# Start addresses of the MLP's weight blocks, modulo 256 bytes, in an attention and MLP kernel on one core

## The chip, the cores and the metric

The kernel runs on one core of a Trainium2 chip. The metric is the device time in microseconds (us) of one execution. Engines are named as the profile names them: PE is the matrix engine's matmul, PEld its weight load, DVE, ACT and POOL are the vector, scalar and GpSimd engines, SP issues DMAs. SBUF is the on-chip memory of 128 partitions; an address here is a byte offset inside a partition.

## What is computed

Eight batches of eight attention heads (576 positions, head size 64), half of the heads with a plain window of 32, half with a dilated one, feed an MLP with 4608 tokens, model size 512 and inner size 2048:

```python
def _attn_ref(q, k, v):
    scores = scale * np.matmul(q, k.transpose(0, 1, 3, 2))
    mask_plain = (rel >= 0) & (rel < window)                                  # window 32
    mask_dil = (rel >= 0) & (rel < window * dilation) & (rel % dilation == 0)  # dilation 4
    scores = np.where(masks[None, :, :, :], scores, -1000000000.0)
    attn = np.exp(scores - np.max(scores, axis=-1, keepdims=True))
    attn = attn / (np.sum(attn, axis=-1, keepdims=True) + 1e-09)
    return np.matmul(attn, v).astype(np.float32)

def _moe_ref(x, w_in, w_out):
    h = x @ w_in
    g = np.where(h >= 1, h, np.where(h <= -1, 0.0, (h + 1) ** 2 / 4.0))
    return (g @ w_out).astype(np.float32)
```

The weights arrive as 64-bit floats.

## The kernel before, in words

The MLP takes nearly all of the time. Its tokens are cut into 9 tiles of 512, its inner size into 16 blocks of 128. One pair (token tile t, inner block f) is a step; there are 144 steps, and `steps` lists them with f running fastest. A step has two parts on PE:

- `layer1` (matmuls on line 670): 4 chunks of 128 model rows, 3 matmuls each. The stationary operand is a piece of 128 columns of block `wi{f}`, the moving operand is 512 columns of the token tile `xh` or `xl`. Every operand is in the fp32r type and split into a high and a low part, so that one product takes three matmuls: high times high, low weight times high token, high weight times low token.
- `layer2` (line 726): 4 blocks of 128 tokens, 3 matmuls each. Here the activations `gh` and `gl` are stationary (128 columns), and the block `wo{f}` is moving (512 columns).

So each step has 24 matmuls of 512 columns, each with a weight load of 128 columns of its own, and 144 steps have 3,456 of them. Between the two parts, DVE and ACT make the activations of a step (`clamped`, `squared`, `activated`, `g_high`, `g_low`, lines 678 to 697); `layer2` runs two steps behind `layer1`, so that PE does not wait for them. Attention of later batches is worked in between steps: score matmuls (`scores_split`, line 336) with a stationary operand of 96 columns from `qs` and a moving one of 256 columns from `kk`, and the values matmuls (line 628). They come from the table `slots`; the first 18 steps and the first heads are in an order written out by hand, `OPENING`, which holds for all engines.

The weights stay in SBUF for the whole run: 32 blocks, `wi0` to `wi15` and `wo0` to `wo15`, of 4,096 bytes in each partition. `fetch` (line 188) allocates a block's place and loads the raw 64-bit numbers from SP; five conversion operations on ACT, DVE and POOL (`scaled`, `low_bits`, `joined`, `high_part`, `low_part`) turn it in place into two fp32r parts. Before a block is fetched, seventeen of the places serve early heads (`home`, `borrow`).

Where a tile lies follows from the sizes of the tiles allocated ahead of it, rounded up to 32 bytes. In the kernel before, almost every tile is a multiple of 256 bytes long (`kr` is 32 numbers longer than it need be; the two tiles `c` of line 282 have 32 numbers beyond the scores, of which 18 are used, and are 3,200 bytes long each, 6,400 together). As a result every block `wi` and `wo`, every token tile `xh` and `xl`, and `gh`, `gl`, `kk` and `qs` begin at 64 modulo 256.

Below, the distance of a matmul pair is the start of a stationary operand minus the start of the moving operand that streams while it is loaded, modulo 256. Pieces inside a tile lie at multiples of 512 bytes, so for the matmuls of `layer1` and `layer2` the distance is 0 throughout. In a score block the second weight load (384 bytes on) stands at 128 to the moving operand of the first matmul.

Of the kernel before, what the change touches and what calls it, by code (L numbers as in the profile page):

```python
# [23 lines left out]
F32 = mybir.dt.float32  # L24
F32R = mybir.dt.float32r
U32 = mybir.dt.uint32
# [5 lines left out]
DM, DF = 512, 2048  # L32
WIN, DIL = 32, 4
QT, NQ = 96, 6
# [62 lines left out]
def body(ctx, tc, q, k, q2, k2, v, v1, fixed_in, w_in, w_out, out):  # L97
# [4 lines left out]
    pool = ctx.enter_context(tc.tile_pool(name="pool", bufs=1))  # L102
# [16 lines left out]
    home = {  # L119
# [3 lines left out]
    }  # L123

    def borrow(name):
        return pool.tile([128, 2 * DM], F32, tag=home[name], name=f"{name}_place")

    first_tiles = 3
    first_q, first_k = first_tiles * QT, first_tiles * QT + 32
# [8 lines left out]
    def load_q(n):  # L138
        if f"q{n}" in home:
            qr = borrow(f"q{n}")[:, :S]  # L140
        else:
            tag = "qs" if n < native and n % 4 else "qr"
            qr = pool.tile([128, S], F32, tag=tag, name=f"qr{n}")
        if n < native:
            some = slice(0, first_q if n == 0 else S)
            nc.sync.dma_start(out=qr[:, some], in_=q[n // 2][:, some])
            whole["q", n] = qr
            for j in range(2):
                heads[n + j]["qs"] = qr[64 * j : 64 * j + 64]
        else:  # L150
            nc.sync.dma_start(out=qr, in_=q2[n - native])
            heads[n]["qr"] = qr

    def load_k(n):
        if f"k{n}" in home:
            kr = borrow(f"k{n}")[:, :KPAD]
        else:
            tag = "kk" if n < native and n % 4 else "kr"
            kr = pool.tile([128, KPAD + 32], F32, tag=tag, name=f"kr{n}")[:, :KPAD]
        if n < native:  # L160
            some = slice(0, first_k if n == 0 else KPAD)
            nc.sync.dma_start(out=kr[:, some], in_=k[n // 2][:, some])
            whole["k", n] = kr
            for j in range(2):
                heads[n + j]["ks"] = kr[64 * j : 64 * j + 64]
        else:
            nc.sync.dma_start(out=kr, in_=k2[n - native])
            heads[n]["kr"] = kr
# [3 lines left out]
    def load_v(n):  # L172
        width = 2 * NQ * (D + 1 if n in late else D)
        if f"v{n}" in home:
            vt = borrow(f"v{n}")[:, :width]
        else:
            vt = pool.tile([128, width], F32, tag="vt", name=f"vt{n}", bufs=2)
        nc.sync.dma_start(out=vt, in_=v1[n // 2] if n in late else v[n // 2])
        vt = vt.rearrange("p (j t d) -> p j t d", j=2, t=NQ)
        for j in range(2):  # L180
            heads[n + j]["vt"] = vt[:, j]

    source = {"wi": w_in, "wo": w_out}
    raws, floats, ready = {}, {}, {}
# [1 line left out]
    cast_by_pool = ('wo0', 'wi2', 'wi3', 'wo2', 'wi12', 'wi0', 'wo11', 'wi13', 'wo1', 'wo12', 'wo15', 'wi10', 'wi8', 'wo14', 'wo8', 'wo6', 'wi6', 'wi15')  # L186

    def fetch(w):
        raw = pool.tile([128, 2 * DM], U32, tag=w, name=f"{w}_raw")
        nc.sync.dma_start(out=raw, in_=source[w[:2]][:, int(w[2:])].bitcast(U32))  # L190
        raws[w] = raw

# [22 lines left out]

    def high_part(w):
        del raws[w]
        ready[w] = pool.tile([128, 2, DM], F32R, tag=w, name=w)
        copy = nc.gpsimd.tensor_copy if w in cast_by_pool else nc.scalar.copy
        copy(out=ready[w][:, 0], in_=floats[w].bitcast(F32))  # L220

    def low_part(w):
# [3 lines left out]
        )  # L226

    convert = {"a": scaled, "b": low_bits, "j": joined, "h": high_part, "l": low_part}


# [44 lines left out]
    def begin(n):  # L275
        hd = heads[n]
        if "c" in hd:
            return
        if f"c{n}" in home:
            both = borrow(f"c{n}")[:QT]  # L280
        else:
            both = pool.tile([QT, NQ * 128 + 32], F32, tag="c", name=f"c{n}", bufs=2)
        hd["c"] = both[:, : NQ * 128].rearrange("p (t j) -> p t j", t=NQ)
        hd["st"] = both[:, NQ * 128 : NQ * 131].rearrange("p (k t) -> p k t", k=3)

# [24 lines left out]
    def scores(n, t):  # L310

        begin(n)
        if n >= native:
            return scores_split(n, t)
        t0 = first_tile(n, t)
        if (n, t0) not in scored:
            tag, bufs = bank(n - n % 2)
            scored[n, t0] = ps.tile([128, 512], F32, tag=tag, name=f"s{n}_{t0}", bufs=bufs)
            if n == t0 == 0:
                spin(7, scored[n, t0])  # L320
        PE.matmul(
            out=native_view(n, t),
            lhsT=heads[n]["qs"][:, t * QT : (t + 1) * QT],
            rhs=heads[n]["ks"][:, t * QT : t * QT + 128],
            start=True,
            stop=True,
        )
# [40 lines left out]
    def score_block(n, t0):  # L368
        begin(n)
        scores_split(n, t0)  # L370
        with tc.high_priority(offset=100):
            masked(n, t0)
            lowest(n, t0)
            lowest(n, t0 + 1)
# [380 lines left out]
    def play(token):  # L755
        if token == "msk":
            nc.scalar.dma_start(out=fixed[:QT, : 3 * 128], in_=fixed_in[:, : 3 * 128])
        elif token == "mk2":
            nc.sync.dma_start(out=ident, in_=fixed_in[:, 3 * 128 :])
        elif token[:2] in source:  # L760
            fetch(token)
        elif token[1:3] in source:
            convert[token[0]](token[1:])
        else:
            kind = token.rstrip("0123456789.")
            operations[kind](*(int(x) for x in token[len(kind) :].split(".")))
# [135 lines left out]
```

## Time and profile before

| what | value |
|---|---|
| median of 2 runs | 911.37 us (910.78 to 911.96) |
| span of the profiled execution | 910.2 us, 14,483 instructions |
| PE busy | 898.1 us, 99% of the span |
| DVE, ACT, POOL busy | 73%, 54%, 26% |
| matmuls of `layer1` and `layer2` | 1,728 and 1,725, and 6 shorter ones at the very end |

The span runs from the first to the last instruction; the time of a run is about 1 us longer, as the two runs, 0.6 and 1.8 us above the span, show. A busy matmul in the profile lasts from its start to its modelled end and overlaps its neighbours, so the pace of PE is read from the distance between starts, or from the chain of waits, where a run of matmuls is one piece with its length and count.

### The profile page before, as it was taken

The page shows a single profiled execution, that of the slowest core. Times are in us where ns is not written, and L with a number is a line of the kernel's source. Part 1 is how long each engine was busy: PE and PEld are TensorE (multiplying, and loading weights), DVE is VectorE, ACT ScalarE, POOL GpSimd, SP SyncE. Part 2 cuts the span into 40 slices and gives each one's busy share as a digit, 9 for nine tenths or more (in the row PEclk, how much of TensorE's full clock was granted, in tenths as well). Part 3 has the DMA queues.
Part 4 walks back from the last instruction along what each step waited for, and adds up shares of the span by engine and source line. Part 5 has one row for each costly group of instructions (what it writes and reads, how often), then busy time and mean ns, then how long its engine had stood idle before and what let it go on. Part 6 is the DMA issues. An engine that isn't in the chain of part 4 may idle for free.

```text
span 910.2 us, 14483 instructions
## 1 busy us (share of the span) xinstructions
PE 898.1 (99%) x4855; PEld 739.9 (81%) x4855; DVE 667.8 (73%) x1982; ACT 489.3 (54%) x1402; POOL 234.5 (26%) x163
## 2 busy tenths in 40 slices
PE   8999999999999999999999999999999999999998
PEld 7777887888888888888888888888888888888886
DVE  6897888888888888788888888788888643334333
ACT  7899865545555555555655555555545422223222
POOL 4665571313222212232231322221223000000000
PEclk9999999999999999999999999999999999999999
DMA  8991112212321223222221232222321010001001
GB/s 284 401 381 50 49 37 80 78 59 71 99 90 58 66 64 118 72 71 72 76 84 57 71 104 85 60 70 59 118 71 45 1 47 1 1 0 48 1 1 46
DMA packets 31258, 73.86 MB, mean 81 GB/s; under 512 B 3568, under 2 KB 4432, under 8 KB 31184
## 3 DMA queue, kind: packets, MB, share of 16 engines
q1 hardware_dynamic: 30928, 72.66, 24.4%
q8 instruction: 38, 0.62, 0.3%
q14 instruction: 36, 0.29, 0.1%
q10 hardware_dynamic: 256, 0.28, 0.1%
HBM read 63.49 MB, written 9.44 MB: 80 GB/s over the span
## 4 chain that ended last, share of the span: by engine, by line
PE 69%; DVE 12%; ACT 8%; POOL 6%; issue 3%; DMA 1%; SPq 0%; ACTq 0%; DVEq 0%; POOLq 0%
PE h L670 32%; PE acc L726 32%; POOL kk L253 3%; DVE thirds L434 3%; ACT c L386 2%; PE s L336 2%; POOL c L423 2%; DVE gl L697 2%; PE o L628 2%; DVE pt L434 2%; ACT kk L245 1%; ACT y L683 1%; ACT qs L242 1%; DVE c L360 1%; DVE y L680 1%
## 5 line engine op out<-in xcount | busy, mean ns | idle before, releaser
L726 PE MATMUL acc<-wo,gh 128*128 128x512 f32 x1150 | 383.9, 391 | 0.0
L670 PE MATMUL h<-xh,wi 128*128 128x512 f32 x1152 | 358.7, 393 | 1.4 <-DVE gl L697 1.4
L726 PEld LDWEIGHTS acc<-wo,gh 128*128 128x128 f32 x1150 | 216.1, 188 | 44.0
L670 PEld LDWEIGHTS h<-xh,wi 128*128 128x128 f32 x1152 | 208.0, 188 | 40.8 <-DVE gl L697 1.1
L670 PE MATMUL h<-xl,wi 128*128 128x512 f32 x576 | 224.4, 390 | 0.0
L726 PE MATMUL acc<-wo,gl 128*128 128x512 f32 x575 | 224.1, 390 | 0.0
L386 ACT ACTIVATE c<-c 96x128 f32<-96x128 f32 x330 | 128.3, 393 | 128.0 <-DVE c L288 128.0
L683 ACT ACTIVATE y<-y,consts 128x512 f32<-128x512 f32 x144 | 104.2, 724 | 169.3 <-DVE y L680 168.3
L253 POOL TENSOR_TENSOR kk<-kr,kk 128x608 fp32r<-128x608 f32 x48 | 89.0, 1855 | 408.3 <-ACT kk L245 399.7
L686 DVE TENSOR_TENSOR h<-h,y 128x512 f32<-128x512 f32 x144 | 100.6, 699 | 67.1 <-ACT y L683 66.3
L697 DVE TENSOR_TENSOR gl<-h,gh 128x512 fp32r<-128x512 f32 x144 | 99.0, 687 | 50.6 <-ACT gh L693 49.6
L680 DVE TENSOR_SCALAR y<-h 128x512 f32<-128x512 f32 x144 | 98.4, 683 | 48.2 <-PE h L670 47.8
L693 ACT CAST gh<-h 128x512 fp32r<-128x512 f32 x144 | 84.2, 585 | 91.3 <-PE acc L726 76.1
L670 PEld LDWEIGHTS h<-xl,wi 128*128 128x128 f32 x576 | 108.2, 188 | 23.3
L726 PEld LDWEIGHTS acc<-wo,gl 128*128 128x128 f32 x575 | 108.0, 188 | 20.5 <-DVE gl L697 0.2
L423 POOL TENSOR_TENSOR c<-c 96x768 f32<-96x768 f32 x51 | 74.8, 1466 | 28.5 <-DVE c L418 27.9
L288 DVE CUSTOM_DVE_ANT_0 c<-s,c 96x128 f32<-96x128 f32 x288 | 71.0, 280 | 1.1
L360 DVE TENSOR_TENSOR c<-s,fixed 96x256 f32<-96x256 f32 (+1 forms) x168 | 61.3, 376 | 11.2 <-PE s L336 9.6
L386 ACT ACTIVATION_READ_ACCUMULATOR c<-c 96x1 f32 x318 | 59.7, 188 | 0.0
L434 DVE STREAM_TRANSPOSE thirds<-c 32x192 f32<-32x192 f32 x144 | 53.1, 369 | 8.5 <-POOL c L423 6.9
L336 PEld LDWEIGHTS s<-kk,qs 128*96 128x96 f32 x288 | 46.4, 161 | 15.4
L336 PE MATMUL s<-kk,qs 128*96 128x256 f32 x288 | 57.7, 283 | 0.0
(90 smaller groups left out, 675.4 us busy)
## 6 DMA issues: line engine op xcount, KB each, us to landing
kr<-k_in SPq DMA_DIRECT2D x52, 304.0 KB, 3.2
qr<-q_in SPq DMA_DIRECT2D x52, 288.0 KB, 2.8
vt<-v_in SPq DMA_DIRECT2D x29, 384.0 KB, 3.9
out<-out SPq DMA_DIRECT2D x35, 256.0 KB, 3.2
wi_raw<-w_in SPq DMA_DIRECT2D x16, 512.0 KB, 8.8
wo_raw<-w_in SPq DMA_DIRECT2D x16, 512.0 KB, 9.7
v_place<-v_in SPq DMA_DIRECT2D x3, 384.0 KB, 9.7
k_place<-k_in SPq DMA_DIRECT2D x3, 304.0 KB, 5.4
```

Of the source, the lines that this page charges most:

```text
L253: nc.gpsimd.tensor_tensor(out=kk[:, 1], in0=kr, in1=kk[:, 0].bitcast(F32), op=ALU.subtract)
L336: PE.matmul(out=split_view(n, t0)[:, t - t0], lhsT=hd["qs"][:, t * QT : (t + 1) * QT], rhs=hd["ks"][:, :, t * QT : t * QT + 128], start=Tr ...
L386: nc.scalar.activation(out=c[:, t], in_=c[:, t], func=AF.Exp, bias=st[:, 0, t : t + 1], scale=-1.0, **total)
L423: engine.tensor_tensor(out=c, in0=c, in1=spread(factor(n)), op=ALU.mult)
L434: nc.vector.transpose(out=pt_of(n)[r : r + 32, :, 32 * g : 32 * g + 32], in_=heads[n]["c"][32 * g : 32 * g + 32, :, r : r + 32],)
L670: PE.matmul(out=hps[s], lhsT=ready[f"wi{f}"][:, w, 128 * c : 128 * c + 128], rhs=x[:, c], start=c == 0 and i == 0, stop=c == NC - 1 and i ...
L680: nc.vector.tensor_scalar(out=y, in0=hps[s], scalar1=-1.0, scalar2=1.0, op0=ALU.max, op1=ALU.min)
L683: nc.scalar.activation(out=ys[s], in_=ys[s], func=AF.Square, bias=half_t, scale=0.5)
L686: nc.vector.tensor_tensor(out=hps[s], in0=hps[s], in1=ys.pop(s), op=ALU.max)
L693: nc.scalar.copy(out=gs[s][0], in_=hps[s])
L697: nc.vector.tensor_tensor(out=gl, in0=hps.pop(s), in1=gh.bitcast(F32), op=ALU.subtract)
L726: PE.matmul(out=acc[m], lhsT=g[:, r], rhs=w[:, part], start=f == 0 and i == 0, stop=(f == NF - 1 or s == len(steps) - 2 and m == TOK // 12 ...
```

## The change

The blocks `wi0` to `wi13` become 8 numbers (32 bytes) longer, and each begins 0, 8, 16 or 24 bytes into its place, by its number modulo 4. The places for the early heads that use those blocks move in the same way. The two tiles `c` become 8 numbers shorter.

```diff
+    def padded_block(w, kind, name):
+        more, first = (8, 2 * (int(w[2:]) % 4)) if w[:2] == "wi" and int(w[2:]) < 14 else (0, 0)
+        tile = pool.tile([128, 2 * DM + more], kind, tag=w, name=name)
+        return tile[:, first : first + 2 * DM]
+
     def borrow(name):
-        return pool.tile([128, 2 * DM], F32, tag=home[name], name=f"{name}_place")
+        return padded_block(home[name], F32, f"{name}_place")
...
     def fetch(w):
-        raw = pool.tile([128, 2 * DM], U32, tag=w, name=f"{w}_raw")
+        raw = padded_block(w, U32, f"{w}_raw")
...
-        ready[w] = pool.tile([128, 2, DM], F32R, tag=w, name=w)
+        ready[w] = padded_block(w, F32R, w).rearrange("p (k d) -> p k d", k=2)
...
-            both = pool.tile([QT, NQ * 128 + 32], F32, tag="c", name=f"c{n}", bufs=2)
+            both = pool.tile([QT, NQ * 128 + 24], F32, tag="c", name=f"c{n}", bufs=2)
```

No instruction is added, taken away or moved: each engine has the same instructions in the same order as before, with the same tiles and the same shapes. Only addresses differ. Since each longer tile moves all that is allocated after it, the addresses after the change are, modulo 256:

| tile | before | after |
|---|---|---|
| `wi0` to `wi7` | 64 | 64, 136, 48, 120, 0, 72, 144, 184 |
| `wi8` to `wi15` | 64 | 64, 104, 176, 248, 192, 104, 224, 224 |
| `wo0` to `wo7` | 64 | 192, 192, 128, 192, 192, 192, 192, 192 |
| `wo8` to `wo15` | 64 | 96, 64, 96, 224, 96, 224, 224, 192 |
| `xh`, `xl` of token tiles 0, 3, 6 / 1, 4, 7 / 2, 5, 8 | 64 | 128 / 160 / 64 |
| `gh`, `gl` | 64 | 192 |

From this table, in `layer1` the distance stays 0 only for `wi0` and `wi8` with token tiles 2, 5 and 8, which is 6 of the 144 steps; in the other 138 it takes some 25 values. In `layer2` it stays 0 for the eight blocks `wo0`, `wo1`, `wo3` to `wo7` and `wo15`, 72 steps; in the other 72 it is 32 to 224.

## Rows read from the trace of the kernel before

**Rows 1.** The page: busy us (share of the span) by engine, and 40 slices.

```profile
span 910.2 us, 14483 instructions
PE 898.1 (99%) x4855; PEld 739.9 (81%) x4855; DVE 667.8 (73%) x1982; ACT 489.3 (54%) x1402; POOL 234.5 (26%) x163
...
PEclk9999999999999999999999999999999999999999
DMA  8991112212321223222221232222321010001001
```

**Rows 2.** The page: the chain that ended last, by engine and by line.

```profile
PE 69%; DVE 12%; ACT 8%; POOL 6%; issue 3%; DMA 1%; SPq 0%; ACTq 0%; DVEq 0%; POOLq 0%
PE h L670 32%; PE acc L726 32%; POOL kk L253 3%; DVE thirds L434 3%; ACT c L386 2%; PE s L336 2%; POOL c L423 2%; DVE gl L697 2%; PE o L628 2%; DVE pt L434 2%; ACT kk L245 1%; ACT y L683 1%; ACT qs L242 1%; DVE c L360 1%; DVE y L680 1%
```

**Rows 3.** The chain, 725 to 760 us: start us, us, piece and matmuls in it.

```profile
726.93 2.72 PE h L670 x12
729.65 2.72 PE acc L726 x12
732.37 2.72 PE h L670 x12
...
754.13 2.72 PE h L670 x12
756.85 2.72 PE acc L726 x12
```

**Rows 4.** The chain, 30 to 110 us.

```profile
79.00 2.72 PE h L670 x12
81.72 2.72 PE acc L726 x12
84.44 2.72 PE h L670 x12
```

**Rows 5.** Stages: length us, busy us (instructions) by engine, granted clock, DMA share, GB/s.

```profile
75.00:175.00 100.00, 99.00 (x517) 80.61 (x517) 82.70 (x215) 71.03 (x185) 47.49 (x39) 1.00 0.20 64
725.00:775.00 50.00, 50.00 (x222) 41.44 (x221) 21.23 (x33) 13.58 (x21) 0.00 (x0) 1.00 0.06 22
```

**Rows 6.** Timeline of PE at the end, matmuls of 256 columns: start us, us, instruction.

```profile
905.47 0.39 PE L726 MATMUL acc<-wo,gh 128*128 128x512 f32 x1
905.69 0.28 PE L708 MATMUL rest<-wo,gh 128*128 128x256 f32 x1
905.81 0.28 PE L708 MATMUL rest<-wo,gl 128*128 128x256 f32 x1
905.93 0.40 PE L708 MATMUL rest<-wo,gh 128*128 128x256 f32 x2
906.17 0.28 PE L708 MATMUL rest<-wo,gl 128*128 128x256 f32 x1
906.29 0.28 PE L708 MATMUL rest<-wo,gh 128*128 128x256 f32 x1
```

**Rows 7.** Timeline of PE around two score blocks.

```profile
504.80 0.39 PE L726 MATMUL acc<-wo,gh 128*128 128x512 f32 x1
505.02 0.40 PE L336 MATMUL s<-kk,qs 128*96 128x256 f32 x2
505.26 0.62 PE L670 MATMUL h<-xh,wi 128*128 128x512 f32 x2
505.73 0.39 PE L670 MATMUL h<-xl,wi 128*128 128x512 f32 x1
...
508.00 0.40 PE L336 MATMUL s<-kk,qs 128*96 128x256 f32 x2
508.24 0.40 PE L726 MATMUL acc<-wo,gh 128*128 128x512 f32 x1
508.47 0.39 PE L726 MATMUL acc<-wo,gl 128*128 128x512 f32 x1
508.70 0.62 PE L726 MATMUL acc<-wo,gh 128*128 128x512 f32 x2
```

**Rows 8.** Loads of the raw `wi` blocks: issues, who waited for the tile's readiness, landing.

```profile
L190 SPq DMA_DIRECT2D wi_raw<-w_in x16: 327/379/699, 5.2 to 53.9; - x16
...
  DMA wi_raw<-w_in: 0.4, 1
...
DMA to landing us min/median/max: 3.9/8.8/10.4
```

## The prediction

> **What bounds the kernel now.** I read the page's busy times first. PE is busy for 99% of the span and the next engine, DVE, for 73% [rows 1]; the granted clock is at its upper level, 2.4 GHz, in all 40 slices. The chain of waits agrees: 64% of it are the matmuls of the two MLP layers, and no other line has more than 3% [rows 2]. So a change that moves no instruction and only alters addresses can act on the time in one main way, through the pace at which PE streams these matmuls. That pace is to be read from the chain in order of time: a part of 12 matmuls takes 2.72 us, over and over [rows 3], which is 2.72 / 12 = 226.7 ns from one start to the next.
>
> How much of the 226.7 ns is streaming? At the very end the kernel has matmuls of 256 columns with the same 128 weight columns, at distance 0. Their starts run from 905.81 to 906.29 in four intervals [rows 6]: 120 ns each. So 256 more columns cost 106.7 ns, which is 2.4 GHz at one column a cycle, and a matmul of either length carries a fixed 13.3 ns (32 cycles) beside its columns. Over 3,456 matmuls that is 46 us. This fixed part is all that an address could change, unless it adds something new.
>
> **The change part by part.** Nothing is removed or added. What moves is the distance between the weights being loaded and the operand that streams meanwhile. By the table of addresses, 138 of 144 steps in layer 1 and 72 of 144 in layer 2 leave distance 0: (138 + 72) x 12 = 2,520 matmuls. One nanosecond on each is worth 2.5 us.
>
> What does another distance cost? The trace has no MLP matmul at any distance but 0, so I bound it. The nearest row is the score block: its second weight load stands at distance 128, and the two 256-column matmuls take 505.02 to 505.26, that is 0.24 us, or 120 ns each [rows 7], and again 508.00 to 508.24. That is the same 120 ns as at distance 0 [rows 6]. If the fixed part belongs to the matmul, the cost of distance 128 is 0. If it belongs to the weight columns, 96 of them should take 10.0 ns instead of 13.3, and the row reads as +3.3 ns. From above: the two MLP matmuls that follow a score block take 0.47 and 0.46 us [rows 7], on average 232.5 ns, 5.8 ns more than the steady pace. So the pace can be pushed, and 5.8 ns is the slip that these rows show; the whole fixed part paid twice would be +13.3 ns. From below: the fixed part vanishes, -13.3 ns. I take 0, by the row nearest in form, and keep -13.3 and +13.3 as ends: -33.5 to +33.5 us.
>
> A second row speaks for 0. Between 79 and 87 us the part of 12 takes the same 2.72 us [rows 4] in a stage in which DVE is busy for 83%, ACT for 71% and POOL for 47% of the time [rows 5], as it does between 725 and 760 us [rows 3], where POOL is idle and DVE and ACT are at 42% and 27% [rows 5]. Those engines read and write SBUF at their own rates, so that their addresses sweep past PE's at every distance modulo 256. None of it shows in PE's pace.
>
> On two reading ports the Trainium skill has a rule ("TensorE: Matmul & The Clock Gate", Part 2, step 1): matmul's moving operand and the weight load have independent read ports, and loading the next weights takes no read bandwidth from the running matmul. By it the distance is worth nothing, as in my forecast. The same page (Part 1) puts back-to-back matmuls of 512 columns at 215.7 ns, and the trace does not agree: 226.7 ns. The 10.9 ns between them are not explained by that page, and a rule that leaves 10.9 ns open cannot exclude that they are a collision of the two reads.
>
> The other edits: the longer blocks and shorter `c` leave every other engine's instructions with the same shapes. Their starts become 8, 16 or 24 bytes off for some blocks; those operations lie beside PE's work, and DVE, the busiest, has 27% of the span idle [rows 1]. I cost them at nothing; without that cover, what could come through is what the chain has outside PE. The 16 loads of raw `wi` blocks land in 8.8 us in the middle, and the waits recorded for them are 0.4 us in one place [rows 8]. If the new starts made each of 14 loads a tenth slower, 0.9 us, this one wait would become 1.3 us; bounds 0 and +1 us, and I take 0.
>
> On line crossings the skill ("SBUF — State Buffer", the cachelines note) says that SBUF is read in lines of 16 bytes and that each new line costs something. The seven odd blocks `wi1` to `wi13` now start 8 bytes into such a line, and 128 weight columns touch 33 lines instead of 32. As an estimate, if the fixed 13.3 ns [rows 3, 6] were nothing but 32 line crossings, one more is 0.4 ns, and 7 x 9 x 12 = 756 matmuls make 0.3 us. No row here shows a start off a 16-byte line.
>
> Sum: 0 on 2,520 matmuls, 0 elsewhere. The profiled span of 910.2 us stays, and with it the median, which lies 1.2 us above that span: 911.4 us.
>
> **The rivals.** *Collisions at other distances (slower).* Place: the weight load of line 670 against the moving `xh`, `xl`, and of line 726 against the moving `wo`. At distance 0 the two reads go through the memory in step; at others the load may hit the part that the moving operand is being read from, and the stream halts. For it: the pace does slip, by 5.8 ns, after score blocks [rows 7], without any engine to wait for; the fixed 13.3 ns are unexplained. Against it: 120 ns at distance 128. Price: 5.8 x 2,520 = 14.6 us, giving 926.0 us; it decides (over 2%, 18.2 us) from 18.2 / 2.52 = 7.2 ns for each changed matmul. Its end is 944.9 us.
>
> *Distance 0 is the collision (faster).* Place: the same. The fixed 32 cycles equal one cycle for each 16 bytes of the 512 that a weight load reads, which is what reads in step would cost. For it: the equal 32 cycles at 256 and 512 columns, both at distance 0 [rows 3, 6]. Against it: at distance 128 it is not smaller [rows 7]. Price: if half of the changed matmuls lost all of it, -13.3 x 1,260 = -16.8 us, giving 894.6; if all did, 877.9 us.
>
> *The opening pays.* Weight loads and conversions with odd starts come late in the first 110 us, where DMA is at 80 to 90% at first [rows 1]. For it: DVE and ACT hold 12% and 8% of the chain [rows 2]. Against: 0.4 us of waiting for these loads in all [rows 8]. If ACT, DVE and POOL each passed on 1 us, 914.4 us.
>
> The change does do what it says: half of the `wo` blocks stay at distance 0, which is already in the 2,520.
>
> **How the numbers follow.** No effect of the distance: 0.53. Slower by collisions: 0.30, spread from 913 to 945 with its middle at 926, so that about 0.13 of it lies over 2%, and I add 0.02 for prices that no row bounds. Faster: 0.12, spread from 878 to 910, of which 0.07 lie over 2%. The opening: 0.05, within 2%. 2% is about what a measurement of this kernel can tell from no change. So faster 0.07, within 2% 0.78, slower 0.15. The range reaches into both: 898 leaves some 0.08 below it and 931 some 0.12 above it. The forecast's own range is 909 to 914.
>
> **What would show it right or wrong.** In the profile after, the chain's parts of 12 matmuls between 725 and 900 us should still read 2.72 us, whatever block they use. If the rival is right, parts differ by block: those of line 726 with `wo0`, `wo1`, `wo3` to `wo7` and `wo15` stay at 2.72 us while others, and nearly all of line 670, are longer (2.79 us at +5.8 ns) or shorter (2.56 us without the fixed part). Parts that are longer only before 110 us would mean the opening. I am wrong if the steady stage's pace depends on the block at all by more than 1 ns.

## The result, and the profile after

The changed kernel takes 920.68 us (920.54 to 920.82, 2 runs) against 911.37 us: a ratio of 1.0105, 95% interval 1.0076 to 1.0134. The profiled span goes from 910.2 to 918.8 us. So it is slower by 9.3 us, 1.0%: inside the range of 898 to 931 us and within 2%, but outside the forecast's own 909 to 914 us and clear of no change, which was the likeliest case of the prediction. What came has the sign, the places and the rough size of the rival of collisions at other distances.

The page looks nearly the same as in [rows 1]. No engine's share moves by more than a point; only PE's busy time is 10 us longer.

```profile
span 918.8 us, 14483 instructions
PE 907.9 (99%) x4855; PEld 738.3 (80%) x4855; DVE 669.6 (73%) x1982; ACT 490.8 (53%) x1402; POOL 232.9 (25%) x163
...
PEclk9999999999999999999999999999999999999999
DMA  8981103212322213222321232221321010001001
```

The difference is in the chain in order of time, the view of [rows 3]. The lines of this kernel are numbered 5 higher: 675 is `layer1`, 731 is `layer2`. First a stretch of token tile 7, then one of token tile 8.

```profile
728.98 2.79 PE acc L731 x12
731.77 2.81 PE h L675 x12
734.58 2.80 PE acc L731 x12
737.39 2.78 PE h L675 x12
740.16 2.73 PE acc L731 x12
742.89 2.80 PE h L675 x12
745.69 2.75 PE acc L731 x12
748.44 2.78 PE h L675 x12
751.23 2.77 PE acc L731 x12
...
862.23 2.73 PE acc L731 x12
864.96 2.73 PE h L675 x12
```

In [rows 3] every piece of 12 matmuls took 2.72 us. Here they take 2.73 to 2.81 us, by block. The shortest are at distance 0: `wo15` at 740.16 and `wo5` at 862.23, and `wi8` with token tile 8 at 864.96. The long ones stand at other distances: `wo13` and `wo14` (224) at 728.98 and 734.58, `wi0` with token tile 7 (160) at 731.77, `wi2` (144) at 742.89. `wi8` is a block whose length, too, was changed, and with a token tile at distance 0 its piece is as short as any here. But distance 0 alone does not bring back 2.72 us: `wo0` at 745.69 takes 2.75 and `wo1` at 751.23 takes 2.77, both at distance 0. Their first weights are loaded while the last matmul of the layer 1 piece ahead streams, and that pair, at the seam of the two layers, stands at 32. The seam ahead of `wo15` stands at 32 as well and leaves less behind.

I also worked out the time between neighbouring starts for all MLP matmuls of both traces, matched one to one with the program's addresses. Of the MLP pairs within a layer, 1,452 in layer 1 and 775 in layer 2 have left distance 0 (intervals over 245 ns, in which PE waits for something else, left out). Their means are 232.1 and 233.3 ns, so 5.4 and 6.6 ns above 226.7. In the kernel before, the same pairs average 227.7 and 227.4 ns, since some stand behind score blocks or other breaks; against that the change costs them 4.3 and 6.0 ns. All such intervals between MLP matmuls add up to 736.3 us before and 749.4 us after: 13.1 us lost in the streams. Of it 10.9 us are on these pairs, 0.9 us on moved pairs at the seams, and 1.3 us on pairs that stayed at distance 0. The span grew by 8.6 us only; where the other 4.5 us went is told below.

### The profile page after: what moved, and what is told of

Same layout as the page of the kernel before. It is cut to its first block, busy times and chain, and to the rows that moved or that the text cites. A ratio compares the mean times of both kernels' runs of the same rounds, so it can differ in the third digit from the quotient of the medians.

```text
span 918.8 us, 14483 instructions
## 1 busy us (share of the span) xinstructions
PE 907.9 (99%) x4855; PEld 738.3 (80%) x4855; DVE 669.6 (73%) x1982; ACT 490.8 (53%) x1402; POOL 232.9 (25%) x163
## 4 chain that ended last, share of the span: by engine, by line
PE 93%; DVE 3%; DMA 1%; issue 1%; ACT 1%; POOL 1%; SPq 0%; DVEq 0%; POOLq 0%
PE h L675 43%; PE acc L731 42%; PE s L341 4%; PE o L633 3%; PE s L326 1%; DMA q_place<-q_in 1%; DVE c_place L293 1%; PE o L545 1%; DMA qr<-q_in 0%; POOL c_place L428 0%; PE t L475 0%; DVE thirds L217 0%; DVE y L685 0%; DVE gl L702 0%; DVE pt L439 0%
## 5 line engine op out<-in xcount | busy, mean ns | idle before, releaser
L731 PE MATMUL acc<-wo,gh 128*128 128x512 f32 x1150 | 387.9, 394 | 0.0
L675 PE MATMUL h<-xh,wi 128*128 128x512 f32 x1152 | 363.2, 396 | 1.3 <-DVE gl L702 1.3
L675 PE MATMUL h<-xl,wi 128*128 128x512 f32 x576 | 227.0, 394 | 0.0
```

The costliest lines, as they stand in the source:

```text
L675: PE.matmul(out=hps[s], lhsT=ready[f"wi{f}"][:, w, 128 * c : 128 * c + 128], rhs=x[:, c], start=c == 0 and i == 0, stop=c == NC - 1 and i ...
L731: PE.matmul(out=acc[m], lhsT=g[:, r], rhs=w[:, part], start=f == 0 and i == 0, stop=(f == NF - 1 or s == len(steps) - 2 and m == TOK // 12 ...
```

## The experiments

Times of before are those measured beside each run on the same chip, and ratios are given with their 95% interval.

**Absolute starts.** Everything is moved by 32 bytes; no distance changes.

```diff
-    consts = const.tile([128, 16], F32, name="consts")
+    consts = const.tile([128, 24], F32, name="consts")
```

> The kernel before with one constant tile 32 bytes longer, so that every tile behind it begins at 96 instead of 64 modulo 256, with all distances as before (0 in both layers). Theory (the distance between the weights being loaded and the moving operand sets the pace): no change, 911.4 us, parts of 12 matmuls of 2.72 us throughout. Rival (the absolute start of an operand sets it, 96 being a bad one, as where the changed kernel has wo8, wo10 and wo12): about 7 ns on all 3,456 matmuls, some 24 us, about 935 us.

Measured: 910.73 us against 910.78 us, ratio 1.0006 (0.9996 to 1.0015). Pieces of 12 take 2.72 us:

```profile
727.29 2.72 PE h L670 x12
730.01 2.72 PE acc L726 x12
```

So where the operands lie does not matter by itself, at least between 64 and 96.

**Layer 2 alone at distance 96.**

```diff
-        y = ys[s] = pool.tile([128, TOK], F32, tag="y", name=f"y{s}")
+        y = ys[s] = pool.tile([128, TOK + 24], F32, tag="y", name=f"y{s}")[:, :TOK]
```

> The kernel before with tile y 96 bytes longer, so that gh and gl begin 96 bytes later: layer 2 alone stands at distance 96 for the 13 blocks wo0 to wo5 and wo8 to wo14, and at 0 for wo6, wo7 and wo15, which move along; layer 1 stays at 0. Theory: 1,380 pairs leave distance 0, by the 7.4 ns that the changed kernel's trace shows for distance 96 in layer 2 (234.1 against 226.7 ns) 10.2 us in the sum, of which 1 to 3 us may go into waits that were there before: 918.5 to 921.6 us; parts of line 726 are 2.81 us with the 13 blocks and 2.72 us with the other three. Rival (only the layer 1 blocks with their odd starts cost anything): 911.4 us.

Measured: 920.02 us against 910.78 us, ratio 1.0102 (1.0087 to 1.0117). One number in one tile, the width of a tile that no matmul reads, costs as much as the whole change. It moves `gh` and `gl`, and with them `wo6`, `wo7` and `wo15`. The chain of this run, in token tile 8:

```profile
817.52 2.81 PE acc L726 x12
820.33 2.73 PE h L670 x12
823.07 2.81 PE acc L726 x12
825.87 2.73 PE h L670 x12
828.61 2.77 PE acc L726 x12
...
867.38 2.78 PE acc L726 x12
```

Layer 2 takes 2.81 us at distance 96, layer 1 at distance 0 takes 2.73. At 828.61 the block is `wo15`, which stands at distance 0 again, and it takes 2.77, not 2.72 (`wo6`, at 867.38, 2.78). The piece ahead of it is layer 1 at distance 0; what stands at 96 is the one pair at the seam, the weights of `gh` at 160 loaded while `xl` at 64 streams. Behind that pair the matmuls of `wo15` start at uneven intervals of 224 to 236 ns and are back at 227 only with the last two. A layer 1 piece behind a piece at 96 has its seam at distance 0 and is back after three. So a disturbed pair costs also what it leaves to the next piece.

**Layer 1 alone at distance 96, in a third of the token tiles.**

```diff
-            both = pool.tile([128, NC * TOK], F32, tag=f"{part}2", name=f"pts_{part}")
+            both = pool.tile([128, NC * TOK + (24 if part == "xl" else 0)], F32, tag=f"{part}2", name=f"pts_{part}")
```

> The kernel before with the second early tile (the place of xl2) 96 bytes longer, so that all weights begin 96 bytes later against xh and xl of token tiles 2, 5 and 8, and everything else keeps its distance: layer 1 at distance 96 in 48 steps (556 pairs), at 0 in the others, layer 2 at 0. Theory: 7.3 ns on 556 pairs, 4.1 us: 914 to 915.5 us; parts of line 670 are 2.81 us in token tiles 2, 5 and 8 alone. Rival (only layer 2 costs, where the moving operand is the weight block): 911.4 us.

Measured: 915.25 us against 910.78 us, ratio 1.0049 (1.0034 to 1.0064). The chain, first in token tile 7 (distance 0), then in token tile 8 (distance 96):

```profile
725.50 2.72 PE acc L726 x12
728.22 2.72 PE h L670 x12
...
820.80 2.81 PE h L670 x12
823.60 2.73 PE acc L726 x12
```

Both layers pay alike, whether the moved block is the stationary operand (layer 1) or the moving one (layer 2).

**Layer 1 at distance 120.** The changed kernel's trace has 39 matmuls at distance 120 that run at 226.7 ns once the first few of their pieces are past, so I had taken 120 for a second good distance.

```diff
+            for part in ("xh", "xl"):
+                more, first = {"xh": (8, 2), "xl": (88, 58)}[part] if t % 3 == 2 else (0, 0)
+                x = pool.tile([128, NC * TOK + more], F32R, tag=f"{part}{t % 3}", name=f"{part}{t}")
+                made.append(x[:, first : first + NC * TOK].rearrange("p (c j) -> p c j", c=NC))
```

> As the run before, but with distance 120 instead of 96 in layer 1 of token tiles 2, 5 and 8 (xh2 and xl2 begin at 72, the weights at 192 modulo 256). Theory with single good distances (in the changed kernel's trace the steps at distance 120 run at 226.7 ns, as at 0): 911.4 us, parts of 2.72 us throughout. Rival (every distance but 0 costs about the same): 914 to 915.5 us.

Measured: 915.39 us against 910.78 us, ratio 1.0051 (1.0034 to 1.0068). The theory of good distances by themselves falls: the matmuls at 120 average 233.3 ns.

```profile
821.13 2.80 PE h L673 x12
823.92 2.76 PE acc L729 x12
826.69 2.80 PE h L673 x12
```

The difference to the changed kernel is where the 8 bytes are. There the weights began 8 bytes into a 16-byte line (at 248 or 184) and the moving operand on one (128 or 64); here it is the moving operand that begins off a line (72), and the weights on one (192). The start inside a line does not do it alone either: other blocks of the changed kernel with weights 8 bytes into a line run at 230 to 233 ns (`wi5` at distance 168 at 233.3). Nor is 120 the only distance with a short interval: `wi2`, on a line, stands at 240 in token tiles 2, 5 and 8 and runs at 227.2 ns past the first matmuls of its pieces; `wi6`, also at 240 in token tiles 1, 4 and 7, at 228.4.

**One block at 120, and at 128.** Everything at distance 0 but `wi7`, which begins 120 bytes later (30 numbers), in the second run 128 bytes (32 numbers); the tile is 256 bytes longer so that nothing else shifts.

```diff
+        more, first = (64, 30) if w == "wi7" else (0, 0)
```

> The kernel before with wi7 alone begun 120 bytes later in a tile 256 bytes longer, all else at distance 0: layer 1 with wi7 at distance 120, its weights beginning 8 bytes into a 16-byte line, the moving operand on one, as in the steps at 120 of the changed kernel. Theory A (distance together with the start inside a line): matmuls with wi7 settle at 226.7 ns as in the changed kernel. Theory B (distance alone; the run at 120 in token tiles 2, 5 and 8, where the moving operand began 8 bytes into a line, settled at 233.3 ns): 233 ns with wi7. The total moves by at most 0.6 us in either case, so the pace is read from the trace.

> As the run before with 8 bytes more, wi7 at distance 128 and both operands on a 16-byte line. Both theories: matmuls with wi7 at about 232 ns, as the changed kernel has at 128; if they were at 226.7 ns too, a single block between blocks at distance 0 would be too short a stretch to show a pace of its own.

Measured, one run each: 910.52 and 911.04 us. The chain around `wi7` in token tile 8, first of the run at 120, then of the run at 128:

```profile
850.56 2.72 PE h L675 x12
853.28 2.72 PE acc L731 x12
```

```profile
850.96 2.80 PE h L675 x12
853.75 2.75 PE acc L731 x12
```

At 120, with the weights 8 bytes into a line, `wi7` runs exactly as at 0 and leaves nothing to the next piece. Eight bytes further on, at 128 and on the line, the piece takes 2.80 us and the next one 2.75. Theory B falls: distance 120 is as good as 0 here and costs the full price in the run before this one. So theory A holds for 120: what counts is the distance together with where in its line each operand begins. Both stretches are 12 matmuls between blocks at 0, so a single block is enough to show its pace.

**The changed kernel without its odd starts.**

```diff
-        more, first = (8, 2 * (int(w[2:]) % 4)) if w[:2] == "wi" and int(w[2:]) < 14 else (0, 0)
+        more, first = (8, 0) if w[:2] == "wi" and int(w[2:]) < 14 else (0, 0)
```

> The changed kernel with the 8, 16 and 24 bytes of offset left out: wi0 to wi13 are still 32 bytes longer, so all starts are multiples of 32 and layer 1 takes the distances 0, 32, 64, 96, 128, 160, 192 and 224; layer 2 as in the changed kernel. Theory (distance): as the changed kernel or little better, 918.5 to 921 us. Rival (the starts off a 16-byte or 32-byte boundary are what costs in layer 1): layer 1 goes back to 226.7 ns a matmul, about 5 us less than the changed kernel, 914.5 to 916 us.

Measured: 921.47 us against 911.38 us, ratio 1.0111 (1.0096 to 1.0126), as slow as the changed kernel. The 8-, 16- and 24-byte offsets are not what costs; starts at multiples of 32 do it. With all starts on lines, this run gives the cleanest table of pace by distance (layers 1 and 2, matmuls with at least four others of their layer ahead): 228.5 ns at 0, 233.2 at 32, 233.4 at 64, 234.0 at 96, 232.5 at 128, 233.8 at 160, 229.3 at 192, 233.3 at 224. Distance 0 is above 226.7 here by what the pairs at the seams leave behind. At one distance the pace hardly depends on the moving operand's start: at 32 it is 233.2, 233.3 and 232.8 ns for starts at 64, 128 and 160.

**The two tiles c alone**, 24 instead of 32 numbers, nothing else:

```diff
-            both = pool.tile([QT, NQ * 128 + 32], F32, tag="c", name=f"c{n}", bufs=2)
+            both = pool.tile([QT, NQ * 128 + 24], F32, tag="c", name=f"c{n}", bufs=2)
```

> The kernel before with the two tiles c 32 bytes shorter each, the other part of the change alone: layer 1 takes distance 192 in token tiles 2, 5 and 8 (452 pairs) and 64 for wi8 and wi9 in the others (128 pairs), layer 2 distance 192 for wo8 (98 pairs). Theory: by the changed kernel's paces (229.5 ns at 192, 233.3 ns at 64) 1.3 + 0.8 + 0.3 us: 912.5 to 914 us. Rival (c matters by itself, or not at all): 911.4 us, all parts 2.72 us.

Measured: 915.65 us against 911.38 us, ratio 1.0047 (1.0030 to 1.0063): 4.3 us, more than the 1.1 to 2.6 us expected. The direct part was priced too low: the moved pairs within a layer lose 3.1 us, not 2.4. Distance 192 runs at 230.9 ns in layer 1 here, not at the 229.5 expected (64 at 233.3, as expected); with the same two starts, 0 and 64, the run without odd starts has 228.8. So one distance does not have one pace in every stream. And I had left out the aftermath: layer 2 pairs at distance 0 average 228.5 ns in this run, against 227.3 for the same 1,444 pairs in the kernel before, which is 1.8 us. In all the streams lose 5.5 us, of which 4.3 came through.

**Half the weight columns.**

```diff
+                half = t < NT - 1 and f < NF - 1 and i > 0
                 PE.matmul(
-                    out=acc[m],
-                    lhsT=g[:, r],
+                    out=acc[m][:64] if half else acc[m],
+                    lhsT=g[:, 128 * m : 128 * m + 64] if half else g[:, r],
```

> As the layer 2 run at distance 96, but in token tiles 0 to 7 and blocks 0 to 14 the second and third matmul of layer 2 load 64 instead of 128 weight columns; half of the rows miss these two products. Blocks wo6 and wo7 are the control at distance 0. Theory (the cost is paid for each weight column that is read beside the stream): of the 7.4 ns the two halved loads keep 3.7 ns, so that a part of line 726 with wo0 is longer than one with wo6 by 0.06 us. Rival (the cost is paid for the 512 moving columns, whatever is loaded): longer by 0.09 us, as with full loads.

Measured in one run: 918.9 us, span 917.1. The kernel leaves two of three products out for half of the rows in these steps. Inconclusive. At distance 96 a piece of layer 2 does get shorter with the halved loads, 2.77 to 2.78 us in token tiles 0 to 7 against 2.81 in token tile 8, where loads are full. But the control was none: `wo7`, at distance 0, takes 2.77 us with halved loads and also with full ones, in token tile 8:

```profile
871.80 2.77 PE acc L727 x12
```

Its first pair, at the seam, stands at 96, as in the run on layer 2 alone. Against an undisturbed piece of 2.72 us the piece at 96 is longer by 0.06 us with halved loads and by 0.09 with full ones, which is what the theory wants; but what halved loads at distance 0 take in an undisturbed stream was not measured.

**Scores at distance 0 too.**

```diff
-                pool.tile([128, 2, KPAD], F32R, tag="kk", name=f"kk{n}"),
+                pool.tile([128, 2 * KPAD + 64], F32R, tag="kk", name=f"kk{n}")[:, 32 : 32 + 2 * KPAD].rearrange("p (a j) -> p a j", a=2),
```

> The kernel before with kk begun 128 bytes later in a tile 256 bytes longer, so that the score matmuls too stand at distance 0 (before: the second weight load of a score block and the one behind it at 128); the MLP is untouched. Theory (distance, score blocks included): the five intervals around a score block took 933 ns where 2,048 columns and five fixed parts make 920; the 13 ns go, on 144 blocks 1.9 us: about 909 us, and the two matmuls behind a score block start 226.7 ns apart. Rival (the longer intervals behind a score block come from the change of shape, 96 weight columns and 256 moving ones): no change, 910.8 to 911.4 us.

Measured: 912.45 us against 911.24 us, ratio 1.0015 (1.0006 to 1.0024): slightly slower, where a gain of 1.9 us was expected. The timeline of PE behind a score block, as in [rows 7]:

```profile
504.78 0.39 PE L336 MATMUL s<-kk,qs 128*96 128x256 f32 x2
505.01 0.63 PE L670 MATMUL h<-xh,wi 128*128 128x512 f32 x2
505.47 0.39 PE L670 MATMUL h<-xl,wi 128*128 128x512 f32 x1
505.70 0.63 PE L670 MATMUL h<-xh,wi 128*128 128x512 f32 x2
506.17 0.39 PE L670 MATMUL h<-xl,wi 128*128 128x512 f32 x1
506.40 0.63 PE L670 MATMUL h<-xh,wi 128*128 128x512 f32 x2
506.86 0.39 PE L670 MATMUL h<-xl,wi 128*128 128x512 f32 x1
507.09 0.62 PE L670 MATMUL h<-xh,wi 128*128 128x512 f32 x2
```

The two score matmuls themselves are faster, 504.78 to 505.01, 115 ns each against 120. But the stream behind them has not settled after two matmuls: for eight matmuls, from 505.01 to 506.86, it runs at 231 ns, and it is back at 226.7 with the ninth, on the mean of all 144 blocks too. In the kernel before it was back from the third. So my reading of the slip behind score blocks as a matter of their own distance falls.

The edit also does not do what I took it to do. The moving operand of a score matmul is not one stretch: its 256 columns are two parts of 128 in `kk`, and the second begins 2,432 bytes behind the first (`KPAD` is 608 numbers), which is 128 modulo 256. In the kernel before, the first 128 columns stand at 128 to the next weights and the last 128 at 0; in this run the first stand at 0 and the last at 128. The run exchanges the two halves. What a score block at distance 0 throughout would do, no run shows.

## Why the prediction came out as it did

*What bounds the kernel* held: no instruction moved, the pace of PE changed, and the time followed that pace, net of the waits told below.

*"I take 0, by the row nearest in form"* is the step that failed. The row was the pair of score matmuls at distance 128, 120 ns each [rows 7], equal to distance 0 [rows 6]. The pace at 128 is not 0 ns but 5 to 6 ns higher (232 ns, the runs without odd starts and with `wi7` at 128). The row was not what it was taken for, in two ways. Only half of its moving columns stand at 128 and the other half at 0, as the last experiment showed; the description ahead of the prediction gives the distance of the first half alone. And 120 ns is not the least that this pair takes: with `kk` moved by 128 bytes the same two matmuls take 115 ns each. So its match with the 120 ns of [rows 6], where loads are of 128 columns, did not show a price of 0. The prediction had named such a reading ("+3.3 ns") and set it aside; on 2,520 matmuls it makes 8.3 us. Nor do two matmuls of 256 columns after a long stretch at distance 0 show a settled pace: a row of two could bound nothing about a stream of twelve.

*The range* held because the rival had a share in it. The mechanism behind the forecast's own 911.4 us, no effect, did not come.

*The busy-engines argument* [rows 4, 5] was true and beside the point: other engines' traffic does not show in PE's pace, but the distance between PE's own two operands does. With the same instructions it moves a matmul from 226.7 to 234 ns (layer 2 at 96). The Trainium skill's rule of two independent read ports ("TensorE: Matmul & The Clock Gate", Part 2, step 1) gave the same answer as the forecast. As a statement on time it does not hold here.

*The rival of collisions* had the right place, in both layers, and nearly the right price for a changed matmul. It took 5.8 ns from [rows 7]; the changed pairs cost 4.3 and 6.0 ns. That the slip behind score blocks has the same size is luck as far as the runs show, since what makes that slip stayed open. Its sum of 14.6 us is close to the 13.1 us that the streams lost, of which 1.3 us stand on pairs that it left at distance 0. The time grew by only 9.3 us, and the profiled span by 8.6, since 4.5 us came back elsewhere, which that sum left out:

- In the kernel before, PE waited in the middle of the values matmuls for DVE's `gl`; five intervals there last 0.42 to 0.58 us, and with the slower stream none is over 0.13. DVE then arrives in time. Intervals inside the values matmuls add up to 3.0 us less. The waits of the weight loads, in the kernel before:

```profile
PEld o L628 <- DVE gl L697: 2.6, 6, 0.5
```

No such line stands in the answer for the changed kernel.

- The first MLP matmul starts 0.8 us earlier, which is not the change's doing. In the profile before, the granted clock was at its lower level, 1.2 GHz, between 8.4 and 11.7 us (0.50 of full speed in the first row below); in the profile after it stayed at the upper one (second row). 24 score matmuls that begin at 8.2 us take 2.76 us in the one and 1.55 us in the other. Ahead of them PE had waited for loads of `q` and `k`, 1.23 and 0.62 us before, 0.80 and 0.59 us after. The first run above, with all starts shifted and all distances as before, has a clock of 0.56 there too, so the dip comes without the change:

```profile
8.40:11.70 3.30, 3.30 (x28) 3.02 (x27) 1.99 (x19) 2.87 (x14) 0.80 (x1) 0.50 1.05 374
```

```profile
8.40:11.70 3.30, 2.92 (x37) 2.58 (x35) 2.94 (x29) 3.29 (x16) 1.58 (x2) 1.00 1.05 397
```

- The two intervals that begin with a score matmul add up to 0.5 us less over the 144 blocks.

- From the first MLP matmul to 110 us, where PE waits for attention's other engines, the streams lose 0.6 us and only 0.3 of it comes through: the first matmul with `wi12` starts at 110.68 us before and at 110.13 after.

Behind 150 us, where PE is busy throughout, the loss builds up to the end.

*The faster rival* fell: in no run and at no distance tried does a stream of the MLP settle below 226.7 ns, so none of them gave back any of the fixed 32 cycles.

*The opening* cost nothing: the `wi` loads land in 9.0 us in the middle, against 8.8 [rows 8]. Nor do the odd starts show in the time: without them the kernel is as slow. The Trainium skill says that each access that crosses to a new 16-byte line pays a penalty ("SBUF — State Buffer", the cachelines note); for weights that begin off a line no run here shows one (`wi7` at 120, 2.72 us). But where in a line an operand begins does matter, as the two runs at 120 show.

What stays open is the mechanism below this; that the two reads collide is the rival's picture of it, which no run tests. The runs show that the pace depends on the distance of the two operands, on the starts inside a line, and on the state in which the preceding matmuls leave the stream. Whether it is paid for each weight column, the halved loads could not settle.

## What to carry to other kernels

Where PE streams without a gap, look at the starts of the weight tile and of the moving tile modulo 256 in pairs, and at those across the seam from one group of matmuls to the next: a padding of a few numbers in an unrelated tile can cost 1% with no instruction changed. Keep tiles at multiples of 256 bytes in length so that all stay at distance 0, or test a distance with one block before moving all; read its pace from the length of a dozen matmuls in the chain, not from two, and check that an operand which streams in several parts has them all at that distance. And price a slower stream net of the waits that it swallows.

## What the runs showed that I had not expected

- Distance 120 is as good as 0 when the weights begin 8 bytes into a line (12 matmuls in 2.72 us) and not when the moving operand does (2.80 us).
- A disturbed stretch is not over with its last matmul: in the run with layer 2 at 96, pieces at distance 0 take 2.73 us where the seam ahead of them is at 0, and 2.77 or 2.78 where the one pair at the seam is at 96 or 160, instead of 2.72; and with the halves of `kk` exchanged a score block leaves eight matmuls at 231 ns.
- A single tile's width, 24 instead of 32 numbers in a softmax tile that no fp32r matmul reads, costs 4.3 us by what it does to the addresses behind it.
